# K of a cached attention block loaded by transposing DMAs instead of transposed on TensorE

## The chip, the cores and the metric

One core of one Trainium2 chip runs the whole program. The metric is the device time of one execution in microseconds (us), here the median of the runs shown. A profile of one execution shows what each engine did: TensorE (PE; its weight loads are listed apart as PEld), VectorE (DVE), ScalarE (ACT), GpSimd (POOL), SyncE (SP, which only issues loads), and the 16 DMA engines that move data between HBM and the on-chip memory (SBUF).

## The reference

Two independent blocks A and B of the same shape, whose outputs are laid side by side. In each, 16 batches of 64 queries attend to a cache of 512 keys in 32 heads of 128 dimensions; all data is bf16:

```python
q = (x @ wq).reshape(B, Sq, H, Dh).transpose(0, 2, 1, 3)     # x: 16 x 64 x 640
scores = einsum("bhqd,bhkd->bhqk", q, k_cache) * Dh ** -0.5   # k_cache: 16 x 32 x 512 x 128
p = softmax(scores, axis=-1)
o = einsum("bhqk,bhkd->bhqd", p, v_cache)                     # v_cache: 16 x 32 x 512 x 128
y = o.transpose(0, 2, 1, 3).reshape(B, Sq, H * Dh) @ wo       # wo: 4096 x 640
```

The two caches of the two blocks are the bulk of the traffic: K is 2 x 16 x 32 x 512 x 128 x 2 bytes = 134.2 MB, V as much. The scores need K with the head dimension on the partitions, while the cache holds one key after another.

## The kernel before

A pass is one block and one half of its heads (16 of 32); there are four passes. In a pass the kernel goes over the eight pairs of batches, and within a pair over the 16 heads, two heads at a time. Such a step of two heads (index `m`; the code calls the single head `g`) is the unit of all work: 4 passes x 8 pairs x 8 steps = 256 steps. The two batches of a pair share the 128 rows of a tile, 64 queries each.

One step does, in this order of dependence:

- KX on TensorE (line 433): two groups, one for each batch, of eight transposes of 128x128, from the loaded K tile `kn_ring` into PSUM; KE on VectorE (line 442) copies each group into `ktp_ring`.
- QP2 (line 451): ten matmuls project the two heads' queries from the transposed input; QE2 on ScalarE scales and copies them to `qT_ring`.
- SM2 (line 467): four matmuls, for two heads and two batches, make the scores; their moving operand is 512 columns of `ktp_ring`.
- MX on VectorE (line 476) takes the negated row maximum, EX on ScalarE (line 482) the exponential with its row sum, RC2 on VectorE (line 488) the reciprocal.
- NM on GpSimd (line 496) multiplies by the reciprocal and writes `pn_ring`, permuting the keys on the way: K is loaded with key 8p + t in partition p, V with key 4p + t, so the scores' columns stand in another order than V's rows.
- TR2 (line 505): eight transposes of the probabilities; TE2 on VectorE (line 512) copies them out.
- PV2 (line 524): sixteen matmuls with V; OE2 on ScalarE (line 532) copies out.
- OP2 (lines 540 and 545): the output projection, summed in PSUM over the heads of a pass; its end is added up in line 560 and stored by a DMA on ScalarE's queue (line 566).

The order on each engine is a fixed template that is repeated with the steps: `PE_T`, `ACT_T`, `DVE_T`, `POOL_T`. Each entry has an offset, which says how many steps ahead of the present one it works: TensorE does KX for step k + 4, SM2 for k + 3, TR2 and PV2 for k + 1 and OP2 for k. An engine takes its instructions strictly in that order.

All loads go through one queue, SP's. `build_plan` orders them by when they are needed (its durations `DMA_NS` serve that order alone), and each waits for its buffer to come free. K and V come in chunks of four heads and one batch, 512 KB each (lines 626 and 622), two DMAs for each of them per chunk; a chunk serves two steps. Both have rings of five chunks (`NKB`, `NVB`). A K buffer comes free when the last reader of its chunk, KX before, has passed. K's source is read in runs of eight keys (2 KB), V's in runs of four (1 KB):

```python
# K, lines 624 to 626
src = blocks[blk][1][2 * bp + j, h0 + hlo:h0 + hhi].rearrange("(hp hs) (p t) d -> (hs p) hp t d", hs=2, t=8)
ins = e.dma_start(kn_ring[:, c % NKB, j, hlo // 2:hhi // 2], src)
# V, lines 621 and 622
src = blocks[blk][2][2 * bp + j, h0 + hlo:h0 + hhi].rearrange("g (p t) d -> p g t d", p=128)
ins = e.dma_start(v_ring[:, c % NVB, j, hlo:hhi], src)
```

Of the kernel before, what the change touches and what calls it, by code (L numbers as in the profile page):

```python
# [5 lines left out]
BF16 = mybir.dt.bfloat16  # L6
F32 = mybir.dt.float32
ACTF = mybir.ActivationFunctionType
ALU = mybir.AluOpType
# [5 lines left out]
class Cfg:  # L15
    G = 4
    HH = 16
    NKB = 5
    NVB = 5
    NX = 2  # L20
    NXN = 1
    XLEAD = 10
    NQ = 2
    NKT = 2
    NP = 4
    NPN = 3
    NT = 2
    NO = 2
    NR = 8
    PE_T = (("TR2", 1), ("QP2", 4), ("KX", 4, 0), ("SM2", 3), ("PV2", 1), ("XT", 0), ("OP2", 0), ("KX", 4, 1))  # L30
    ACT_T = (("QE2", 4), ("OE2", 1), ("XE", 0), ("EX", 3, 0), ("EX", 3, 1), ("OV", 0), ("ST", -1))
    DVE_T = (("TE2", 1), ("RC2", 2), ("KE", 4, 0), ("MX", 3, 0), ("MX", 3, 1), ("KE", 4, 1), ("OVF", 0))
    POOL_T = (("NM", 0, 0), ("NM", 0, 1))
    TAIL_SPLIT = 2
    SLOT_NS = 3600.0
# [3 lines left out]
class Op:  # L39
# [3 lines left out]
    def __init__(self, eng, kind, idx, reads=(), writes=(), dur=0.0, ts=None, aux=None):  # L43
# [12 lines left out]
        self.dma = kind in ("LDK", "LDV", "LDX", "LDWQ", "LDWO", "ST")  # L56


STAGES = ("LDW", "LDX", "LDK", "LDV", "KX0", "KE0", "KX1", "KE1", "QP2", "QE2", "SM2", "MX0", "MX1", "EX0", "EX1",
          "RC2", "NM0", "NM1", "TR2", "TE2", "XT", "XE", "PV2", "OE2", "OP2", "OV", "ST")  # L60
STAGE_IDX = {s: i for i, s in enumerate(STAGES)}
SUB_KINDS = ("KX", "KE", "EX", "NM", "MX")


def build_plan(dims, cfg):
    NBLK, B, H = dims["NBLK"], dims["B"], dims["H"]
    G = cfg.G
# [23 lines left out]
    def mk(eng, kind, idx, reads, writes, stage, m_ts, sub=0, aux=None, dur=0.0):  # L91
        return Op(eng, kind, idx, reads, writes, dur=dur, aux=aux, ts=(m_ts, STAGE_IDX[stage], sub))

    OFF = {}
    for t in cfg.PE_T:
        OFF.setdefault(t[0], t[1])

    def make_op(kind, m, sub):
        g0, g1 = 2 * m, 2 * m + 1
        ps_, bp, grp, h0 = step_info(g0)  # L100
        c = g0 // G
        if kind == "KX":
            return mk("pe", "KX", (m, sub), [("kn", c % cfg.NKB, g0 % G), ("kn", c % cfg.NKB, g1 % G), ("ident",)],
                      [("KTB",)], "KX%d" % sub, m, sub)
        if kind == "KE":
            return mk("dve", "KE", (m, sub), [], [("KTB",), ("ktp", m % cfg.NKT, sub)], "KE%d" % sub, m, sub)
        if kind in ("MX", "EX", "NM"):
            g = 2 * m + sub
            r = g % cfg.NR
# [18 lines left out]
        if kind == "QE2":  # L128
            return mk("act", "QE2", m, [], [("QB",), ("qT", m % cfg.NQ)], "QE2", m)
        if kind == "SM2":  # L130
            return mk("pe", "SM2", m, [("qT", m % cfg.NQ), ("ktp", m % cfg.NKT, 0), ("ktp", m % cfg.NKT, 1)],
                      [("SB", 0), ("SB", 1)], "SM2", m)
        if kind == "RC2":
            return mk("dve", "RC2", m, [("rowsum", r0), ("rowsum", r1)], [("recip", r0), ("recip", r1)], "RC2", m)
# [29 lines left out]

    templates = {"pe": cfg.PE_T, "dve": cfg.DVE_T, "pool": cfg.POOL_T, "act": cfg.ACT_T}
    for eng, tmpl in templates.items():
        offs = [t[1] for t in tmpl] + [cfg.XLEAD]
        for k in range(-max(offs), NMAC - min(offs)):
            for t in tmpl:
                kind, off = t[0], t[1]  # L170
                sub = t[2] if len(t) > 2 else 0
                if kind in ("XT", "XE"):
                    op = make_op(kind, k, 0)
# [3 lines left out]
                m = k + off  # L177
                if 0 <= m < NMAC:
                    op = make_op(kind, m, sub)
# [167 lines left out]
def mha_kernel(nc, blocks, out, cfg=None):  # L347
    cfg = cfg or Cfg()
# [14 lines left out]
    prune_waits(progs)  # L363
    NBP, SPB, NHALF = info["NBP"], info["SPB"], info["NHALF"]
    HH = SPB
    NKB, NVB, NX, NXN, NQ, NKT, NP, NPN, NT, NO, NR = (cfg.NKB, cfg.NVB, cfg.NX, cfg.NXN, cfg.NQ, cfg.NKT, cfg.NP,
                                                       cfg.NPN, cfg.NT, cfg.NO, cfg.NR)

    def step_info(g):
        grp = g // SPB  # L370
# [7 lines left out]
    with contextlib.ExitStack() as es:  # L378
        block = es.enter_context(nc.Block())

        def sb(name, shape, dt):
            return es.enter_context(nc.sbuf_tensor(name, shape, dt))
# [15 lines left out]
        negmax = sb("negmax", [128, NR], F32)  # L398
        rowsum = sb("rowsum", [128, NR], F32)
        recip = sb("recip", [128, NR], F32)  # L400
        ones_sb = sb("ones_sb", [128, 128], BF16)
        ident = sb("ident", [128, 128], BF16)
        ps = es.enter_context(nc.psum_tensor("ps", [128, 8, 512], F32))
# [9 lines left out]
        else:  # L413
            out_ps_all = ps[:, 0, 0:DN]
        S_BANK0 = 2
        PT_BANK, O_BANK, Q_BANK, KT_BANK = 4, 5, 6, 7
# [4 lines left out]
        kt_ps_flat = ps[:, KT_BANK, :].bitcast(BF16)  # L421
        kt_ps = kt_ps_flat.rearrange("p (t s) -> p t s", t=8)

        def s_bank(sub):
            return ps[:, S_BANK0 + sub, :]

        def em_KX(e, op):
            m, j = op.idx
            g0 = 2 * m
            c, hp = g0 // G, (g0 % G) // 2  # L430
            first = last = None
            for t8 in range(8):
                ins = e.transpose(kt_ps[:, t8, :], kn_ring[:, c % NKB, j, hp, t8, :], ident[:, :])  # L433
                first = first or ins
                last = ins
            return first, last

        def em_KE(e, op):
            m, j = op.idx
            src = kt_ps_flat.rearrange("p (t hs pp) -> p t hs pp", t=8, hs=2)  # L440
            dst = ktp_ring[:, m % NKT, :, j, :].rearrange("p hs (t pp) -> p t hs pp", t=8)
            ins = e.tensor_copy(dst, src)  # L442
            return ins, ins

        def em_QP2(e, op):
            m = op.idx
# [15 lines left out]
        def em_SM2(e, op):  # L462
            m = op.idx
            first = last = None
            for sub in range(2):
                for j in range(2):
                    ins = e.matmul(s_bank(sub)[64 * j:64 * j + 64, :], qT_ring[:, m % NQ, sub, 64 * j:64 * j + 64],  # L467
                                   ktp_ring[:, m % NKT, sub, j, :], start=True, stop=True, tile_position=(0, 64 * j))
                    first = first or ins
                    last = ins  # L470
            return first, last
# [19 lines left out]
        def em_NM(e, op):  # L491
            g = op.idx
            r = g % NR
            src = p_ring[:, g % NP, :].rearrange("q (th tl pp) -> q th tl pp", th=2, tl=4)
            dst = pn_ring[:, g % NPN, :].rearrange("q (tl pp th) -> q th tl pp", tl=4, th=2)
            ins = e.tensor_scalar(dst, src, recip[:, r:r + 1], 1.0, ALU.mult, ALU.mult)  # L496
            return ins, ins

        def em_TR2(e, op):
# [116 lines left out]
        def em_LDKV(e, op):  # L616
            c, j, hlo, hhi, _piece = op.aux
            blk, bp, grp, ps_, hh0 = step_info(c * G)
            h0 = (ps_ % NHALF) * HH + hh0
            if op.kind == "LDV":  # L620
                src = blocks[blk][2][2 * bp + j, h0 + hlo:h0 + hhi].rearrange("g (p t) d -> p g t d", p=128)
                ins = e.dma_start(v_ring[:, c % NVB, j, hlo:hhi], src)
            else:
                src = blocks[blk][1][2 * bp + j, h0 + hlo:h0 + hhi].rearrange("(hp hs) (p t) d -> (hs p) hp t d",
                                                                              hs=2, t=8)
                ins = e.dma_start(kn_ring[:, c % NKB, j, hlo // 2:hhi // 2], src)  # L626
            return ins, ins

        emitters = dict(KX=em_KX, KE=em_KE, QP2=em_QP2, QE2=em_QE2, SM2=em_SM2, MX=em_MX, EX=em_EX, RC2=em_RC2,
                        NM=em_NM, TR2=em_TR2, TE2=em_TE2, PV2=em_PV2, OE2=em_OE2, OP2=em_OP2, OV=em_OV,  # L630
                        OVP=em_OVP, OVF=em_OVF, ST=em_ST, XT=em_XT, XE=em_XE, INIT1=em_INIT1, INIT2=em_INIT2,
                        LDWQ=em_LDWQ, LDWO=em_LDWO, LDX=em_LDX, LDK=em_LDKV, LDV=em_LDKV)
# [87 lines left out]
```

## Time and profile before

| | |
|---|---|
| median of two runs | 958.89 us (958.25 and 959.54) |
| span of the profiled execution | 956.8 us, so 1.4 to 2.7 us of a run's time lie outside it |
| TensorE busy | 919.4 us |
| VectorE busy | 841.9 us |
| ScalarE busy | 567.1 us |
| GpSimd busy | 416.9 us |
| moved on SP's queue | 294.69 MB, 91.0% of the 16 DMA engines' span |
| K loads | 256 of 512 KB (the last chunk's four halves are 256 KB each), median 7.0 us to landing in block A and 4.8 in B |
| V loads | the same number and sizes, 7.2 and 5.7 us |

Busy times are sums over instructions; TensorE's matmuls are pipelined, so that the sum of their durations is larger than the time in which they follow each other: a group of eight K transposes is busy 0.61 us from its first start to its last end, and starts 0.45 us ahead of whatever follows it. In the groups of instructions the columns are the line, engine and operation, the output and the inputs, the count, the busy time, the mean in ns, and the idle time before them with what ended it. The chain of waits is followed back from the last instruction of the program; its shares tell where the time of the path that ended last went.

### The profile page before, as it was taken

To read this page: it belongs to the slowest core of one execution; us is meant where nothing else is said; L and a number is where in the kernel's file an instruction comes from. 1 tells how busy PE (TensorE), PEld (TensorE's weight loads), DVE (VectorE), ACT (ScalarE), POOL (GpSimd) and SP (SyncE) were. 2 spreads that over 40 slices of the span, in tenths; PEclk is the share of its full clock that TensorE was granted. 3 is DMA by queue.
4 is the path that set the end of the run, shared out by engine and by line. 5 is a ranking of instruction groups with operands and counts; after the bars stand their busy time and mean duration, and the time that the engine had idled before them with its cause. 6 is when DMAs were issued, how large, how long until landed. Compare 5 with 4: busy or idle time off the path is not lost.

```text
span 956.8 us, 34351 instructions
## 1 busy us (share of the span) xinstructions
PE 919.4 (96%) x14755; PEld 733.5 (77%) x15008; DVE 841.9 (88%) x1552; ACT 567.1 (59%) x1585; POOL 416.9 (44%) x518
## 2 busy tenths in 40 slices
PE   4999999999999999999999999999999999999997
PEld 3877777778777777877777787777877778777775
DVE  2898899898899999899999899889899998999996
ACT  1666656666665565656566666666666656565654
POOL 0444444444444444444444444444444444444443
PEclk9999999999999999999999999999999999999999
DMA  9999999999999999888999999988888988899830
GB/s 315 364 365 364 351 365 367 365 368 351 338 337 337 343 330 315 299 292 305 322 332 352 326 353 327 306 294 296 302 305 288 308 301 297 295 297 314 295 124 15
DMA packets 230871, 299.51 MB, mean 313 GB/s; under 512 B 9536, under 2 KB 165184, under 8 KB 230720
## 3 DMA queue, kind: packets, MB, share of 16 engines
q1 hardware_dynamic: 228416, 294.69, 91.0%
q8 instruction: 118, 1.93, 0.8%
q10 hardware_dynamic: 2304, 2.62, 0.8%
q14 instruction: 33, 0.27, 0.1%
HBM read 294.65 MB, written 2.62 MB: 311 GB/s over the span
## 4 chain that ended last, share of the span: by engine, by line
PE 89%; DVE 4%; POOL 3%; issue 2%; SPq 1%; DMA 1%; POOLq 0%; DVEq 0%
PE ps L433 22%; PE ps L524 14%; PE ps L451 14%; PE ps L467 14%; PE ps L505 12%; PE ps L545 7%; PE ps L540 5%; POOL pn_ring L496 3%; DVE out_sb L560 1%; DVE ktp_ring L442 1%; DVE pT_ring L512 1%; PE ps L604 1%; DMA xn_ring<-in_A_x_dram 1%; SPq L626 1%; SPq L583 1%
## 5 line engine op out<-in xcount | busy, mean ns | idle before, releaser
L496 POOL TENSOR_SCALAR pn_ring<-p_ring,recip 128x512 bf16<-128x512 bf16 x512 | 416.3, 843 | 532.7 <-DVE recip L488 532.7
L442 DVE COPY ktp_ring<-ps 128x1024 bf16<-128x1024 bf16 x512 | 353.7, 691 | 105.3 <-PE ps L433 85.1
L482 ACT ACTIVATE p_ring<-ps,negmax 128x512 bf16<-128x512 f32 x512 | 345.6, 684 | 4.8 <-DVE negmax L476 4.8
L476 DVE TENSOR_REDUCE negmax<-ps 128x1 f32<-128x512 f32 x512 | 327.3, 681 | 0.4 <-PE ps L467 0.3
L433 PE MATMUL ps<-ident,kn_ring 128*128 128x128 bf16 x4096 | 314.6, 220 | 2.8 <-DMA kn_ring<-in_A_k_cache_dram 1.6
L532 ACT ACTIVATE oT_ring<-ps 128x256 bf16<-128x256 f32 x256 | 98.0, 383 | 306.0 <-PE ps L524 306.0
L433 PEld LDWEIGHTS ps<-ident,kn_ring 128*128 128x128 bf16 x4096 | 251.9, 98 | 34.2 <-DVE ktp_ring L442 2.6
L524 PEld LDWEIGHTS ps<-pT_ring,v_ring 128*128 128x128 bf16 x4096 | 133.5, 98 | 109.2 <-issue 100.0
L451 PE MATMUL ps<-xT_ring,wq_sb 128*128 128x128 bf16 x2560 | 186.4, 220 | 3.2 <-DMA wq_sb<-in_A_wq_dram 3.2
L512 DVE COPY pT_ring<-ps 128x1024 bf16<-128x1024 bf16 x256 | 174.5, 682 | 4.6 <-PE ps L505 3.8
L524 PE MATMUL ps<-pT_ring,v_ring 128*128 128x64 bf16 x4096 | 163.8, 194 | 3.3 <-issue 1.7
L467 PE MATMUL ps<-ktp_ring,qT_ring 128*64 128x512 bf16 x1024 | 159.8, 392 | 0.4 <-ACT p_ring L482 0.4
L505 PE MATMUL ps<-ident,pn_ring 128*128 128x128 bf16 x2048 | 156.7, 219 | 3.5 <-POOL pn_ring L496 3.5
L451 PEld LDWEIGHTS ps<-xT_ring,wq_sb 128*128 128x128 bf16 x2560 | 155.2, 98 | 3.5 <-DMA wq_sb<-in_A_wq_dram 3.5
L459 ACT ACTIVATE qT_ring<-ps 128x256 bf16<-128x256 f32 x256 | 98.4, 384 | 66.8 <-PE ps L451 66.8
L505 PEld LDWEIGHTS ps<-ident,pn_ring 128*128 128x128 bf16 x2048 | 124.1, 98 | 7.0 <-POOL pn_ring L496 6.7
L545 PE MATMUL ps<-wo_sb,oT_ring 128*128 128x128 bf16 x512 | 112.1, 219 | 13.4
L482 ACT ACTIVATION_READ_ACCUMULATOR p_ring<-ps,negmax 128x1 f32 x512 | 105.0, 205 | 0.0
L540 PE MATMUL ps<-wo_sb,oT_ring 128*128 128x512 bf16 x259 | 97.8, 379 | 0.0
L540 PEld LDWEIGHTS ps<-wo_sb,oT_ring 128*128 128x128 bf16 x512 | 50.1, 98 | 30.6 <-ACT oT_ring L532 0.3
L467 PEld LDWEIGHTS ps<-ktp_ring,qT_ring 128*64 128x64 bf16 x1024 | 36.1, 108 | 27.1 <-ACT p_ring L482 0.6
L545 PEld LDWEIGHTS ps<-wo_sb,oT_ring 128*128 128x128 bf16 x512 | 50.1, 98 | 0.0
(13 smaller groups left out, 112.7 us busy)
## 6 DMA issues: line engine op xcount, KB each, us to landing
kn_ring<-in_A_k_cache_dram SPq DMA_DIRECT2D x128, 512.0 KB, 7.0
v_ring<-in_A_v_cache_dram SPq DMA_DIRECT2D x128, 512.0 KB, 7.2
kn_ring<-in_B_k_cache_dram SPq DMA_DIRECT2D x126, 512.0 KB, 4.8
v_ring<-in_B_v_cache_dram SPq DMA_DIRECT2D x126, 512.0 KB, 5.7
wq_sb<-in_A_wq_dram SPq DMA_DIRECT2D x8, 640.0 KB, 10.4
wo_sb<-in_A_wo_dram SPq DMA_DIRECT2D x8, 640.0 KB, 10.2
wq_sb<-in_B_wq_dram SPq DMA_DIRECT2D x8, 640.0 KB, 8.4
wo_sb<-in_B_wo_dram SPq DMA_DIRECT2D x8, 640.0 KB, 7.5
```

Of the source, the lines that this page charges most:

```text
L433: ins = e.transpose(kt_ps[:, t8, :], kn_ring[:, c % NKB, j, hp, t8, :], ident[:, :])
L442: ins = e.tensor_copy(dst, src)
L451: ins = e.matmul(q_ps[:, sub * 128:(sub + 1) * 128], wq_sb[:, ps_ % 2, kt, hh * DH:(hh + 1) * DH], xT_ring[:, grp % NX, kt, :], start=(kt ...
L467: ins = e.matmul(s_bank(sub)[64 * j:64 * j + 64, :], qT_ring[:, m % NQ, sub, 64 * j:64 * j + 64], ktp_ring[:, m % NKT, sub, j, :], start=T ...
L476: ins = e.reduce_max(negmax[:, r:r + 1], s_bank(g % 2), axis=AX.X, negate=True)
L482: ins = e.activation(p_ring[:, g % NP, :], s_bank(g % 2), ACTF.Exp, bias=negmax[:, r:r + 1], scale=1.0, accum_out=rowsum[:, r:r + 1])
L496: ins = e.tensor_scalar(dst, src, recip[:, r:r + 1], 1.0, ALU.mult, ALU.mult)
L505: ins = e.transpose(pt_ps[:, sub, t, :], pn_ring[:, g % NPN, t * 128:(t + 1) * 128], ident[:, :])
L512: ins = e.tensor_copy(pT_ring[:, m % NT].rearrange("p s t q -> p (s t q)"), pt_ps_flat)
L524: ins = e.matmul(o_ps[:, col:col + 64], v_ring[:, c % NVB, j, gi, t, :], pT_ring[:, m % NT, sub, t, 64 * j:64 * j + 64], start=(t == 0), s ...
L540: ins = e.matmul(out_ps0, oT_ring[:, m % NO, sub, :], wo_sb[:, ps_ % 2, hh, 0:N0], start=(hh == 0), stop=(hh == SPB - 1))
L545: last = e.matmul(out_ps1, oT_ring[:, m % NO, sub, :], wo_sb[:, ps_ % 2, hh, N0:DN], start=(hh == 0), stop=(hh == SPB - 1))
```

## The change

K is loaded by a transposing DMA straight into the layout that the scores need. The source of one DMA is viewed as 512 rows (four heads x 128) of 1 KB, each row four consecutive keys; the destination `kt_ring` has the head dimension on the partitions, and for each of the four positions in a row the 512 rows. So head `gi`'s columns run over (position t, row r) for key 4r + t, which is V's order.

With that, the K transposes (KX) and their copies (KE) go, with the PSUM bank and the ring `ktp_ring` that they used; SM2 reads `kt_ring` directly, as four runs of 128 columns, and waits for the DMA itself; NM writes its result in the order in which it reads it. A K buffer comes free after SM2 (offset 3) instead of KX (offset 4), and the loads are ordered by that. Nothing else in the templates changes.

```diff
-    NKT = 2
+    KR = 128
-    PE_T = (("TR2", 1), ("QP2", 4), ("KX", 4, 0), ("SM2", 3), ("PV2", 1), ("XT", 0), ("OP2", 0), ("KX", 4, 1))
+    PE_T = (("TR2", 1), ("QP2", 4), ("SM2", 3), ("PV2", 1), ("XT", 0), ("OP2", 0))
-    DVE_T = (("TE2", 1), ("RC2", 2), ("KE", 4, 0), ("MX", 3, 0), ("MX", 3, 1), ("KE", 4, 1), ("OVF", 0))
+    DVE_T = (("TE2", 1), ("RC2", 2), ("MX", 3, 0), ("MX", 3, 1), ("OVF", 0))
...
-            return mk("pe", "SM2", m, [("qT", m % cfg.NQ), ("ktp", m % cfg.NKT, 0), ("ktp", m % cfg.NKT, 1)],
+            return mk("pe", "SM2", m, [("qT", m % cfg.NQ), ("kn", c % cfg.NKB, g0 % G), ("kn", c % cfg.NKB, g1 % G)],
...
-        for kind, ring, n_ring, cons, tb in (("LDK", "kn", cfg.NKB, "KX", 2), ("LDV", "v", cfg.NVB, "PV2", 2.5)):
+        for kind, ring, n_ring, cons, tb in (("LDK", "kn", cfg.NKB, "SM2", 2), ("LDV", "v", cfg.NVB, "PV2", 2.5)):
...
+    KR, KJ = cfg.KR, SK // cfg.KR
...
-        kn_ring = sb("kn_ring", [128, NKB, 2, G // 2, 8, DH], BF16)
+        kt_ring = sb("kt_ring", [128, NKB, 2, KJ, G * KR], BF16)
-        ktp_ring = sb("ktp_ring", [128, NKT, 2, 2, SK], BF16)
...
-                ins = e.transpose(kt_ps[:, t8, :], kn_ring[:, c % NKB, j, hp, t8, :], ident[:, :])
...
-            ins = e.tensor_copy(dst, src)
...
+                g = 2 * m + sub
+                c, gi = g // G, g % G
                 for j in range(2):
                     ins = e.matmul(s_bank(sub)[64 * j:64 * j + 64, :], qT_ring[:, m % NQ, sub, 64 * j:64 * j + 64],
-                                   ktp_ring[:, m % NKT, sub, j, :], start=True, stop=True, tile_position=(0, 64 * j))
+                                   kt_ring[:, c % NKB, j, :, gi * KR:(gi + 1) * KR], start=True, stop=True, tile_position=(0, 64 * j))
...
-            src = p_ring[:, g % NP, :].rearrange("q (th tl pp) -> q th tl pp", th=2, tl=4)
-            dst = pn_ring[:, g % NPN, :].rearrange("q (tl pp th) -> q th tl pp", tl=4, th=2)
-            ins = e.tensor_scalar(dst, src, recip[:, r:r + 1], 1.0, ALU.mult, ALU.mult)
+            ins = e.tensor_scalar(pn_ring[:, g % NPN, :], p_ring[:, g % NP, :], recip[:, r:r + 1], 1.0, ALU.mult, ALU.mult)
...
-                src = blocks[blk][1][2 * bp + j, h0 + hlo:h0 + hhi].rearrange("(hp hs) (p t) d -> (hs p) hp t d",
-                                                                              hs=2, t=8)
-                ins = e.dma_start(kn_ring[:, c % NKB, j, hlo // 2:hhi // 2], src)
+                src = blocks[blk][1][2 * bp + j, h0 + hlo:h0 + hhi].rearrange("g (r t) d -> (g r) (t d)", t=KJ)
+                ins = e.dma_start_transpose(kt_ring[:, c % NKB, j, :, hlo * KR:hhi * KR], src)
```

More of the change, by code (lines that the diff above doesn't have):

```diff
@@ L56, in __init__ @@
         self.dma = kind in ("LDK", "LDV", "LDX", "LDWQ", "LDWO", "ST")
-STAGES = ("LDW", "LDX", "LDK", "LDV", "KX0", "KE0", "KX1", "KE1", "QP2", "QE2", "SM2", "MX0", "MX1", "EX0", "EX1",
+STAGES = ("LDW", "LDX", "LDK", "LDV", "QP2", "QE2", "SM2", "MX0", "MX1", "EX0", "EX1",
           "RC2", "NM0", "NM1", "TR2", "TE2", "XT", "XE", "PV2", "OE2", "OP2", "OV", "ST")
 STAGE_IDX = {s: i for i, s in enumerate(STAGES)}
-SUB_KINDS = ("KX", "KE", "EX", "NM", "MX")
+SUB_KINDS = ("EX", "NM", "MX")
 def build_plan(dims, cfg):
@@ L101, in make_op @@
         c = g0 // G
[L102 to L106, printed above, removed]
         if kind in ("MX", "EX", "NM"):
@@ L365, in mha_kernel @@
     HH = SPB
-    NKB, NVB, NX, NXN, NQ, NKT, NP, NPN, NT, NO, NR = (cfg.NKB, cfg.NVB, cfg.NX, cfg.NXN, cfg.NQ, cfg.NKT, cfg.NP,
-                                                       cfg.NPN, cfg.NT, cfg.NO, cfg.NR)
+    NKB, NVB, NX, NXN, NQ, NP, NPN, NT, NO, NR = (cfg.NKB, cfg.NVB, cfg.NX, cfg.NXN, cfg.NQ, cfg.NP,
+                                                  cfg.NPN, cfg.NT, cfg.NO, cfg.NR)
     def step_info(g):
@@ L415, in mha_kernel @@
         S_BANK0 = 2
-        PT_BANK, O_BANK, Q_BANK, KT_BANK = 4, 5, 6, 7
+        PT_BANK, O_BANK, Q_BANK = 4, 5, 6
         pt_ps_flat = ps[:, PT_BANK, :].bitcast(BF16)
@@ L420, in mha_kernel @@
         q_ps = ps[:, Q_BANK, 0:256]
-        kt_ps_flat = ps[:, KT_BANK, :].bitcast(BF16)
-        kt_ps = kt_ps_flat.rearrange("p (t s) -> p t s", t=8)
         def s_bank(sub):
             return ps[:, S_BANK0 + sub, :]
[L427 to L443, printed above, removed]
         def em_QP2(e, op):
@@ L623, in em_LDKV @@
             else:
-                src = blocks[blk][1][2 * bp + j, h0 + hlo:h0 + hhi].rearrange("(hp hs) (p t) d -> (hs p) hp t d",
-                                                                              hs=2, t=8)
-                ins = e.dma_start(kn_ring[:, c % NKB, j, hlo // 2:hhi // 2], src)
+                src = blocks[blk][1][2 * bp + j, h0 + hlo:h0 + hhi].rearrange("g (r t) d -> (g r) (t d)", t=KJ)
+                ins = e.dma_start_transpose(kt_ring[:, c % NKB, j, :, hlo * KR:hhi * KR], src)
             return ins, ins
-        emitters = dict(KX=em_KX, KE=em_KE, QP2=em_QP2, QE2=em_QE2, SM2=em_SM2, MX=em_MX, EX=em_EX, RC2=em_RC2,
+        emitters = dict(QP2=em_QP2, QE2=em_QE2, SM2=em_SM2, MX=em_MX, EX=em_EX, RC2=em_RC2,
                         NM=em_NM, TR2=em_TR2, TE2=em_TE2, PV2=em_PV2, OE2=em_OE2, OP2=em_OP2, OV=em_OV,
```

## The prediction

> **What bounds the kernel now.** I read the page first: busy shares, slices, chain, groups.
>
> ```profile
> span 956.8 us, 34351 instructions
> ...
> PE 919.4 (96%) x14755; PEld 733.5 (77%) x15008; DVE 841.9 (88%) x1552; ACT 567.1 (59%) x1585; POOL 416.9 (44%) x518
> ...
> GB/s 315 364 365 364 351 365 367 365 368 351 338 337 337 343 330 315 299 292 305 322 332 352 326 353 327 306 294 296 302 305 288 308 301 297 295 297 314 295 124 15
> DMA packets 230871, 299.51 MB, mean 313 GB/s; under 512 B 9536, under 2 KB 165184, under 8 KB 230720
> ...
> q1 hardware_dynamic: 228416, 294.69, 91.0%
> ...
> PE 89%; DVE 4%; POOL 3%; issue 2%; SPq 1%; DMA 1%; POOLq 0%; DVEq 0%
> PE ps L433 22%; PE ps L524 14%; PE ps L451 14%; PE ps L467 14%; PE ps L505 12%; PE ps L545 7%; PE ps L540 5%; POOL pn_ring L496 3%; DVE out_sb L560 1%; DVE ktp_ring L442 1%; DVE pT_ring L512 1%; PE ps L604 1%; DMA xn_ring<-in_A_x_dram 1%; SPq L626 1%; SPq L583 1%
> ...
> L442 DVE COPY ktp_ring<-ps 128x1024 bf16<-128x1024 bf16 x512 | 353.7, 691 | 105.3 <-PE ps L433 85.1
> ...
> L433 PE MATMUL ps<-ident,kn_ring 128*128 128x128 bf16 x4096 | 314.6, 220 | 2.8 <-DMA kn_ring<-in_A_k_cache_dram 1.6
> ```
>
> TensorE sets the end: 89% of the chain, its largest line the K transposes, L433. But the loads stand close behind. The slices show some 365 GB/s in the first third and about 300 later, so I next took two stretches as windows (the columns after the busy times are granted clock, DMA share and GB/s):
>
> ```profile
> 100.00:200.00 100.00, 98.53 (x1599) 79.35 (x1626) 89.95 (x168) 62.57 (x175) 44.54 (x56) 1.00 1.07 365
> 700.00:800.00 100.00, 98.03 (x1589) 78.16 (x1614) 90.66 (x169) 59.79 (x169) 44.78 (x56) 1.00 0.89 297
> ```
>
> Early the rings are being filled and the DMA engines give all they have, 365 GB/s at a share above 1. Late they deliver only what TensorE uses. Last, the chain of waits over one steady step, a pair of heads:
>
> ```profile
> 412.93 0.45 PE ps L433 x8
> 413.38 0.45 PE ps L505 x8
> 413.82 0.56 PE ps L451 x10
> 414.38 0.45 PE ps L433 x8
> 414.83 0.55 PE ps L467 x4
> 415.38 0.57 PE ps L524 x16
> 415.95 0.05 issue
> 416.01 0.22 PE ps L545
> 416.23 0.21 PE ps L540
> 416.44 0.06 PE ps L545
> 416.50 0.45 PE ps L433 x8
> ```
>
> One step is 416.50 - 412.93 = 3.57 us, and 256 x 3.57 = 914 us of the 956.8.
>
> **What is removed.** Two groups of eight K transposes, 2 x 0.45 = 0.90 us a step. TensorE alone would need 2.67 us a step, 256 x 2.67 = 684 us, 230 less. VectorE loses L442: 841.9 - 353.7 = 488 us, 1.9 a step; ScalarE needs 567 / 256 = 2.2, GpSimd 417 / 256 = 1.6. All lie below 2.67, so no engine takes TensorE's place. L496 becomes a contiguous normalization; it is the same 512 elements at 843 ns or less or somewhat more, and would have to grow from 1.6 to over 2.67 us a step to matter: nothing. The four score matmuls of L467 read their 512 columns as four runs of 128 instead of one: nothing if the 0.55 us holds, and at worst the pace of L433 (0.45 us for 8 x 128 columns against 0.55 for 4 x 512) says that short runs are not dearer. They now wait for the K landing itself. Queued behind that wait on TensorE are PV, the output projection and the next step, and behind them all evictions; what a late K costs is thus whole, and belongs to the loads below. K buffers come free one step later (scores at offset 3, not transposes at 4), one of the ring's ten steps; with the loads behind, that is not what holds them.
>
> **What takes its place: the loads.** The bytes stay, 294.7 MB on q1. Even at 365 GB/s they need 807 us, more than TensorE's 684. So gain or loss is the price of a transposed byte, which no row of before shows. The trace's DMA packet records give sizes and durations. Medians: 4 B 9 ns (9537 of them), 1024 B 46 ns (V and Wq, 141312), 1280 B 55 ns (x, Wo and stores, 14336), 2048 B 84 ns (K, 65536). They lie on a line: (84 - 46) / 1024 = 0.037 ns per byte, plus 8 ns per packet. Over 16 engines:
> - all but K: (141312 x 46 + 14336 x 55) / 16 = 406 + 49 = 455 us
> - K now: 65536 x 84 / 16 = 344 us.
> Together 799 us, against 807 from the saturated rate: the medians price the load within 1%, and I multiply sums by 1.01.
>
> K's 134.2 MB, transposed, has these prices:
> - **as whole 1 KB source rows** at V's price: 131072 x 46 / 16 = 377 us.
> - **as 256 B pieces.** A head dimension is 128 x 2 B = 256 B. In a 1 KB row four keys stand side by side, and the destination puts them in four different groups, so a row must be cut in four for the transposition. By the line, 8 + 0.037 x 256 = 17.5 ns each, 524288 x 17.5 / 16 = 573 us.
> - **as small writes.** If the destination were served in 32 B pieces at the 9 ns of the smallest packets: 4194304 x 9 / 16 = 2359 us.
>
> The lower end is 344 (nothing lost against now), the upper 2359. I take 573: it is next to the 1 KB and 2 KB rows on the same line, while the upper end has only the 4 B row behind it.
>
> Sum: (455 + 573) x 1.01 = 1038 us of loading. Ends: 1 us before the first issue, 2 for the last landing (the shortest K landing, 3.6 us, less 512 KB at 365 GB/s, 1.4), and the last chunk's work: two steps of about 3.2 at the end of the trace and 5.0 from the last PV (951.8) to 956.8, so 11. That is 1052 of span. Outside the span lie 958.9 - 956.8 = 2.1, so **1054 us**. TensorE then idles 1052 / 256 - 2.67 = 1.4 us a step.
>
> The Trainium skill, "Advanced Engine Details and Errata", section "X-Bar Transpose (TRN2)", states the contrary: transposing DMAs as fast as plain ones, 350 to 400 GB/s; with it K would take 336 to 383 us and the kernel 815 to 862. "DMA: Bandwidth & Descriptors", section "Latency and other measured facts", gives 261 GB/s where a middle dimension is not contiguous, as in these rows; that estimate is 514 us for K and 995 in all. Neither is shown by the trace.
>
> SP issues each transfer. The issues of K (256 packets) and V (512 packets) both take 0.37 us when nothing holds them, so packet count does not show in it. Were the issue to grow as pieces do (2048 against 512), it would be 1.5 us; per chunk 2 x 1.5 + 2 x 0.37 = 3.7 us, hidden under the 8.1 us that a chunk's loads then take. Before,
>
> ```profile
> SPq L626 <- PE ps L433: 353.5, 119, 4.0
> ```
>
> SP waited 353.5 us for TensorE to free K buffers; that wait goes, and SP is held by the DMA engines instead, as in 100 to 200 us. V, Wo and x stand behind K in the same queue, and are late with it.
>
> **Rivals.**
> *Rows move whole* (faster): K at 377. (455 + 377) x 1.01 + 16 = 856 us. For it: 1 KB runs already move at 46 ns for V. Against: the four keys of a row part on the way. It wins under the point where K takes 460 us, 14.0 ns per 256 B piece or 292 GB/s: that gives 940, 2% below 958.9.
> *Something between* (890 to 985): part of the piece's 8 ns is overlapped. The band within 2%, about what a measurement of this kernel can tell from no change, is K between 460 and 498 us.
> *Each transposing DMA drains the engines* before the next transfer starts. 3.6 - 1.4 = 2.2 us of latency exposed, x 256 = 563: 856 + 563 = 1419 or 1054 + 563 = 1617. For it: nothing shown; against it: plain transfers overlap freely (share 1.07).
> *Small writes*: (455 + 2359) x 1.01 + 16 = 2858.
> *A slow TensorE*: after the 4.2 us for which the matmuls stood still before 23.3 us a group of eight transposes took 1.03 us instead of 0.61, until 27 us. At that ratio a step is 2.67 x 1.69 = 4.5 us, 1153 in all. But it cannot stay: at 4.5 against the loads' 4.05 us a step TensorE would never idle, and the pace returned after some 4 us of work. It adds at most at stalls, inside the range.
> *No effect of the removal*: excluded, L433 and L442 are gone by the diff and nothing replaces them on an engine.
>
> The skill's "VectorE: DVE Perf Modes", section "Rules for kernel authors", speaks against the change: for 128 x 128 use TensorE where PSUM will do, the crossbar otherwise; its table has 1309 ns for one by DMA. The 4096 blocks one after another would make 5362 us as an estimate; the trace, with 0.45 us per eight on TensorE, can't say how far DMAs overlap them.
>
> **How the numbers follow.** 256 B pieces, 985 to 1110: 0.33, the likeliest. Whole rows, 835 to 890: 0.26. Between, 890 to 985: 0.12, of it 0.05 faster than 940, 0.06 within 2% and 0.01 slower. Drained, 1110 to 1620: 0.19. Small writes and other steep prices above that: 0.10. Faster is 0.26 + 0.05 = 0.31, same 0.06, slower 0.33 + 0.01 + 0.19 + 0.10 = 0.63. The range goes from 840 to 1560 and leaves out the steep prices, the upper edge of the drained case (0.05) and a little below (0.02). The forecast's own range is 985 to 1110.
>
> **What would show it.** Right: no L433 and L442; packets of 256 B on q1 near 17.5 ns; DMA share 0.9 or more in all slices at 270 to 300 GB/s; the chain mostly DMA into kt_ring and TensorE's busy time near 919 - 315 x 0.73 = 690 (0.73 is the chain's 0.90 us a step over the 1.23 that 314.6 / 256 gives). Wrong: K packets of 1 KB at 46 ns (whole rows); a DMA share far below 0.9 while TensorE waits for K (drained, or SP as the limit, which its issue durations would show); hundreds of thousands of packets under 64 B (small writes).

## The result, and the profile after

The changed kernel takes **1224.94 us** (1223.66 to 1226.22, two runs) against 958.89: ratio 1.278, interval 1.274 to 1.282. It is slower, as forecast, but by 266 us where 95 were forecast. Where the executions of a kernel fall into a faster and a slower state, the times and ratios below are of the faster ones.

From the page of the changed kernel: span, busy times, granted clock, DMA share and GB/s in 40 slices, DMA packets, two DMA queues, and the chain of waits.

```profile
span 1221.9 us, 25784 instructions
...
PE 847.0 (69%) x10784; PEld 586.6 (48%) x10912; DVE 551.0 (45%) x1040; ACT 553.7 (45%) x1585; POOL 350.1 (29%) x518
...
PEclk9878888888888878888988887988888888888888
DMA  9999999999999999999999999999999999999997
GB/s 229 260 244 236 266 251 239 248 247 245 246 259 263 246 253 243 264 238 255 249 240 254 245 244 244 262 240 228 254 237 243 236 237 264 235 253 236 238 248 168
DMA packets 693715, 298.97 MB, mean 245 GB/s; under 512 B 537952, under 2 KB 693600, under 8 KB 693600
...
q1 hardware_dynamic: 691296, 294.70, 107.8%
...
q8 instruction: 86, 1.41, 0.5%
...
SPq 40%; DMA 28%; PE 19%; ACT 9%; issue 2%; POOL 1%; DVE 0%; POOLq 0%; ACTq 0%; DVEq 0%
SPq L600 34%; DMA v_ring<-in_B_v_cache_dram 12%; DMA v_ring<-in_A_v_cache_dram 10%; ACT p_ring L459 7%; PE ps L444 6%; PE ps L499 6%; SPq L597 4%; DMA kt_ring<-in_B_k_cache_dram 3%; DMA kt_ring<-in_A_k_cache_dram 3%; PE ps L426 2%; PE ps L480 2%; PE ps L515 2%; ACT oT_ring L507 2%; SPq L572 1%; ACT xT_ring L587 1%
```

The chain has passed from TensorE to the loads: 40% SP's queue (L600 issues K), 28% DMA. The packets under 512 B are the 256 B pieces. The DMA engines are never without work (share 1.08) and yet carry 245 GB/s. The share adds up the durations of packets, which overlap, and does not say that the engines move all they can: before, a share of 1.07 went with 365 GB/s. SP's issues in order of time (start, duration, operation, destination and source, count):

```profile
304.97 7.88 SPq L600 DMA_TRANSPOSE kt_ring<-in_A_k_cache_dram  x2
312.89 1.13 SPq L597 DMA_DIRECT2D v_ring<-in_A_v_cache_dram  x2
314.06 7.74 SPq L600 DMA_TRANSPOSE kt_ring<-in_A_k_cache_dram  x2
```

SP issues almost without a pause, a transposing DMA holding it some 4 us, and a chunk takes 9 us. The waits of SP's queue name TensorE as what it waits for, 249 us in 92 waits:

```profile
SPq L600 <- PE ps L444: 249.1, 92, 5.4
```

That is an inferred releaser, and wrong here. Set against the end of the last scores that read the buffer, SP's issue of a K load comes 27 to 36 us later (10th to 90th percentile; 24 at the least), of a V load 33 to 39 us later. The buffers are free long before. TensorE in turn uses V 6.2 us (median) after the issue of a chunk's first V load starts, and a V load takes 5.2 us to land. So the stream of loads sets the time, and its sum is what went wrong.

### The profile page after: what moved, and what is told of

Read it like the earlier page. It is cut to its first block, busy times and chain, and to the rows that moved or that the text cites. A ratio compares the mean times of both kernels' runs of the same rounds, so it can differ in the third digit from the quotient of the medians.

```text
span 1221.9 us, 25784 instructions
## 1 busy us (share of the span) xinstructions
PE 847.0 (69%) x10784; PEld 586.6 (48%) x10912; DVE 551.0 (45%) x1040; ACT 553.7 (45%) x1585; POOL 350.1 (29%) x518
## 4 chain that ended last, share of the span: by engine, by line
SPq 40%; DMA 28%; PE 19%; ACT 9%; issue 2%; POOL 1%; DVE 0%; POOLq 0%; ACTq 0%; DVEq 0%
SPq L600 34%; DMA v_ring<-in_B_v_cache_dram 12%; DMA v_ring<-in_A_v_cache_dram 10%; ACT p_ring L459 7%; PE ps L444 6%; PE ps L499 6%; SPq L597 4%; DMA kt_ring<-in_B_k_cache_dram 3%; DMA kt_ring<-in_A_k_cache_dram 3%; PE ps L426 2%; PE ps L480 2%; PE ps L515 2%; ACT oT_ring L507 2%; SPq L572 1%; ACT xT_ring L587 1%
## 5 line engine op out<-in xcount | busy, mean ns | idle before, releaser
L471 POOL TENSOR_SCALAR pn_ring<-p_ring,recip 128x512 bf16<-128x512 bf16 x512 | 349.4, 695 | 864.6 <-DVE recip L465 864.6
L499 PE MATMUL ps<-pT_ring,v_ring 128*128 128x64 bf16 x4096 | 188.9, 205 | 263.0 <-DMA v_ring<-in_A_v_cache_dram 131.1
L444 PE MATMUL ps<-kt_ring,qT_ring 128*64 128x512 bf16 x1024 | 174.8, 424 | 70.1 <-ACT p_ring L459 34.6
L426 PE MATMUL ps<-xT_ring,wq_sb 128*128 128x128 bf16 x2560 | 214.5, 239 | 5.3 <-DMA wq_sb<-in_A_wq_dram 4.9
L480 PE MATMUL ps<-ident,pn_ring 128*128 128x128 bf16 x2048 | 186.4, 243 | 9.9 <-ACT xT_ring L587 8.4
L426 PEld LDWEIGHTS ps<-xT_ring,wq_sb 128*128 128x128 bf16 x2560 | 182.4, 109 | 6.7 <-issue 3.3
L480 PEld LDWEIGHTS ps<-ident,pn_ring 128*128 128x128 bf16 x2048 | 147.6, 111 | 66.5 <-POOL pn_ring L471 20.2
L515 PE MATMUL ps<-wo_sb,oT_ring 128*128 128x512 bf16 x384 | 160.4, 452 | 0.0
L444 PEld LDWEIGHTS ps<-kt_ring,qT_ring 128*64 128x64 bf16 x1024 | 38.7, 113 | 113.1 <-ACT p_ring L459 72.3
L465 DVE RECIPROCAL recip<-rowsum 128x2 f32<-128x2 f32 x256 | 41.6, 162 | 7.4 <-ACT p_ring L459 1.4
```

The source lines that it names most:

```text
L426: ins = e.matmul(q_ps[:, sub * 128:(sub + 1) * 128], wq_sb[:, ps_ % 2, kt, hh * DH:(hh + 1) * DH], xT_ring[:, grp % NX, kt, :], start=(kt ...
L471: ins = e.tensor_scalar(pn_ring[:, g % NPN, :], p_ring[:, g % NP, :], recip[:, r:r + 1], 1.0, ALU.mult, ALU.mult)
L480: ins = e.transpose(pt_ps[:, sub, t, :], pn_ring[:, g % NPN, t * 128:(t + 1) * 128], ident[:, :])
L499: ins = e.matmul(o_ps[:, col:col + 64], v_ring[:, c % NVB, j, gi, t, :], pT_ring[:, m % NT, sub, t, 64 * j:64 * j + 64], start=(t == 0), s ...
L515: ins = e.matmul(out_ps0, oT_ring[:, m % NO, sub, :], wo_sb[:, ps_ % 2, hh, 0:N0], start=(hh == 0), stop=(hh == SPB - 1))
```

## The experiments

Before the runs the theories were: **boundaries**, time lost where the DMA engines pass between transposing and plain transfers; **each transposing DMA**, a price for every one; **strided pieces**, 256 B reads at steps of 1 KB being slow; **coupling**, engines and queue holding each other up. Later came **instruction fetch** and **SBUF traffic**.

### The loads alone

All computing is left out and zeros are stored; SP issues the same loads in the same order, each waiting only for the landing of the load that filled its buffer before. Each time in this part and the next is of one execution.

```diff
-            run_program(sync, progs["sp"])
+            for op in loads:                      # the same list, op.waits: the buffer's earlier load
+                for s, v in op.waits:
+                    e.wait_ge(sems[s], v * 16)
+                _, ins = emitters[op.kind](e, op)
+                ins.then_inc(sems[op.sem], 16)
```

**Plain K**, the list of the kernel before:

> The loads of the kernel before alone, in its order on SP's queue: all computing is left out, each load waits only for the landing of the load that filled its buffer before, and zeros are stored at the end. A gauge for the other three. Every theory: 294.7 MB at the 365 GB/s of the filled stretch, 807 us and about 15 at the ends, 820 us.

Measured 823.7 us. The price list of the prediction, 455 + 344 at the medians, multiplied by 1.01 and with the ends, holds for plain loads.

**Alternating**, the list of the changed kernel:

> The loads of the changed kernel alone, K by transposing DMAs, K and V alternating as there; all computing left out, zeros stored. At the medians of the packet records (18 ns for 256 B, 46 for 1 KB, 56 for 1280 B) the engines need 590 + 406 + 50 = 1046 us; the changed kernel's span is 1222, so 176 us are to be placed. Theory 'boundaries' (time is lost where the DMA engines pass between transposing and plain transfers): about 1210 us. Theory 'each transposing DMA' (something at the start or end of every one): about 1210. Theory 'strided pieces' (256 B read at steps of 1 KB stall in HBM): about 1210. Theory 'coupling' (TensorE's waits for V and SP's waits for K buffers hold each other up, and a slower granted clock): about 1060.

Measured 1168.4 us. Coupling falls: without any computing most of the excess is there.

**Separated**, `loads = [all but LDK] + [all LDK]`:

> The same loads alone with K by transposing DMAs, but all plain loads first and then all K loads: one passage between the kinds instead of some 256. Boundaries: 1050 to 1070 us. Each transposing DMA: about 1210, and K's part about 590 + 176 = 770 us for 256 DMAs, 3.0 us each. Strided pieces: about 1210 too. Coupling: the same as the alternating loads.

Measured 1072.5 us, 96 less. The GB/s in 40 slices, of the separated run:

```profile
GB/s 310 350 351 350 349 349 351 351 349 349 350 352 349 349 349 349 348 236 214 217 216 213 215 213 210 219 224 213 216 236 235 242 232 234 236 242 240 236 231 237
```

and of the alternating one:

```profile
GB/s 228 278 251 261 241 256 262 257 242 249 254 240 255 254 259 250 238 246 255 238 266 270 254 264 257 256 269 246 247 253 252 259 249 275 259 260 269 259 256 264
```

The first 17 slices are plain loads at 350; after the break K comes alone at 210 to 242. By the packet records K takes 599 us (from 461 to 1060), 2.34 us for each 512 KB. In a quarter of a microsecond up to some 285 of its packets start, 14.0 ns per packet and engine, which would be 1.80 us a DMA. So 0.54 us of each is lost inside the K stream, and 96 us more by alternating.

The packet records also show where. K's packets were counted in order of their start, 2048 to a DMA, and the time of each 64 compared with the peak pace, 56.5 ns. In the alternating run a transposing DMA behind V loses 0.94 us, all of it in its first 640 packets; the second of the two, behind another K, loses 0.61 us, of which 0.51 there. In the separated run it is 0.50 us a DMA. So the loss stands at the start of each transposing DMA, and the start is dearer behind V: 256 x (0.77 - 0.50) = 69 of the 96 us.

**Rows of 256 B** (`KR = 512`, so keys in another order than V's; alternating):

> The loads alone, alternating, K by transposing DMAs whose source rows are 256 B (2048 rows a DMA, one key each) instead of 1 KB: the same bytes and pieces, read in order of address. Strided pieces: the loss goes, 1050 to 1070 us or less. Boundaries, and each transposing DMA: unchanged against the 1 KB rows, within 2%. If SP's issue grows with the rows (2048 instead of 512), it is slower than with 1 KB rows.

Measured 1161.7 us, 0.6% below the 1 KB rows. Strided pieces fall, and SP's issue does not grow with the rows (medians 3.51 and 2.88 us in the two blocks, against 3.57 and 2.72).

**One K, one V** (`K0 V0 K1 V1` instead of `K0 K1 V0 V1`):

> The loads alone (computing left out), as in the alternating run of 1168 us, but passing between K and V after every DMA instead of every two: 512 passages between the kinds in the order of issue instead of 260. With all plain loads first it was 1072, so 96 us for 260 passages, 0.37 us each. Boundaries: 512 x 0.37 = 190, about 1262 us. If the 96 us come from something else than the number of passages (the length of what is queued, or the loads of x and the weights between them): 1168 within 2%.

Measured 1137.0 us: no sign of the 94 us more that a fixed price per passage asks for. That it is 31 us less is not shown to come from the order (see the copies below).

**Four K, four V** (the loads of two chunks together):

> The loads alone, with the loads of two chunks together: four of K, then four of V, 128 passages between the kinds instead of 260. If a passage has its price (96 us for 260): 1072 + 47 = 1120 us. If the engines run further apart in a longer run of V and that is what costs (512 passages took 1137): 1168 or more.

Measured 1123.4 us: as a price per passage has it. Against the separated order this is 51 us at 128 passages, 96 at 260 and 65 at 512; the last, with only one V load between two K loads, does not lie on their line.

**Chunks of eight heads**, DMAs of 1 MB:

```diff
-    G = 4
+    G = 8
-    NKB = 5
-    NVB = 5
+    NKB = 2
+    NVB = 2
```

> The loads alone in chunks of eight heads: DMAs of 1 MB, half as many, and two buffers for each of K and V; the order is two K, two V, so passages and bytes between them are as in the order of four and four with 512 KB. Within the K stream of the separated run a DMA took 2.34 us, of which 1.80 at its peak rate. Theory 'each transposing DMA' (0.54 us lost at every one): 128 fewer, 69 us less than the run with four and four. Theory 'along the stream' (the loss goes with bytes): the same time as that one, within 2%.

Measured 1040.0 us, 83 less than four and four, for the same bytes between passages: 83 / 128 = 0.65 us for each transposing DMA saved. This is the clearest of the experiments on the stream. The V loads are half as many too, but the packet records put the loss with K: a 1 MB DMA loses 0.71 us against the peak pace, 0.64 of it in the first 640 of its 4096 packets, where the 512 KB DMAs of four and four lose 0.65. The price is one of the start, and not of the bytes.

**V from ScalarE's queue**:

> The loads alone, with V issued from ScalarE's queue and all others, K's transposing DMAs among them, from SP's, so that both kinds are in flight on every DMA engine at once. If a passage costs because one ring must run empty: 1072 us or less, down to 875, which is the sum of both kinds at their peak rates (285 packets of 256 B in 0.25 us and 94 of 1 KB). If transposing DMAs need all 16 engines in step and every plain packet between them holds all up: 1168 us or more.

Measured 1020.3 us. Between 20 and 520 us V and K packets start one for one (132,000 of each), at 350 GB/s in all; which engine carried which the records don't say. But nothing held V back, so that it ran ahead and the rest was K alone: nearly the separated order. I read it as support for "one ring in order", which the whole kernel then refuted (below).

### What computing adds: 1168 to 1225

**11000 small matmuls beside the alternating loads**:

```diff
+        def _(t):
+            for i in range(11000):
+                t.matmul(ps[0:128, 0, 0:128], ident[:, :], ident[:, :], start=True, stop=True)
```

> The alternating loads alone, with 11000 small matmuls beside them on TensorE whose operands are one constant tile that no load touches: some 22000 instructions to be fetched, as in the changed kernel, and no other work. In the changed kernel's packet records the 256 B packets fall from 0.87 to 0.13 of their full rate for some 1.2 us when an instruction fetch of 16 KB (86 on queue 8) begins. Theory 'instruction fetch' (a fetch holds one DMA engine and a transposing DMA waits for all 16): 1168 + 86 x 0.6 to 0.9 = 1220 to 1245 us. Theory 'coupling' (the 57 us between 1168 and 1225 come from SP and TensorE waiting for each other): 1168 within 1%. Theory 'SBUF traffic': 1168 within 1%.

Measured 1213.1 us, with 86 fetches on queue 8. The matmuls end at 619 us, so the run is its own control. Windows (TensorE, its weight loads and GpSimd with counts, granted clock, DMA share, GB/s):

```profile
40.00:240.00 200.00, 200.00 (x3586) 200.00 (x3584) 0.00 (x0) 1.00 1.13 244
240.00:440.00 200.00, 200.00 (x3586) 200.00 (x3584) 0.00 (x0) 1.00 1.14 235
...
660.00:860.00 200.00, 0.00 (x0) 0.00 (x0) 0.00 (x0) 0.50 1.07 257
860.00:1060.00 200.00, 0.00 (x0) 0.00 (x0) 0.00 (x0) 0.50 1.08 254
```

The rate is 235 to 244 GB/s with the matmuls and 254 to 257 without; the alternating loads alone had 256 and 250 in the first two of these windows, 255 and 259 in the last two. Against its own second part the run so loses some 35 us (6% of 620), though the alternating loads too are 2% slower in the first windows; against the total of the alternating run it is 45.

**22000 waits on a raised semaphore instead of the matmuls** (fetches, no access to SBUF):

> The alternating loads alone, with 22000 waits on a semaphore that has long been raised as the only instructions on TensorE: instructions are fetched as in the run with 11000 matmuls (1213 us), and no engine touches SBUF. Instruction fetch: 1168 + 45 = 1213 us again, with about 86 packets of 16 KB on queue 8. If the 45 us came from TensorE's reads of SBUF: 1168 within 1%.

Measured 1201.0 us, with only 43 fetches (the trace has some 11,000 of the waits). The total alone decides nothing, but the packet records do: averaged over the fetches, q1 falls from 265 GB/s in the microsecond before a fetch to 136 between 0.5 and 1.75 us after its start. Beside the matmuls it falls from 277 to 97. As no engine touches SBUF here, TensorE's reads of SBUF are not what stops the loads.

**Large copies by VectorE, ScalarE and GpSimd**:

> The alternating loads alone, with VectorE, ScalarE and GpSimd copying large tiles inside SBUF that no load touches, 1680 instructions of 1 to 2 us in all, so few fetches. SBUF traffic (the compute engines' accesses slow the transposed writes): 1200 us or more. Instruction fetch and coupling: 1168 within 1.5%.

Measured 1514.5 us, but that is VectorE's copies, which go on long after the loads: the last V packet starts at 1128 us of the span, where it was 1156 in the alternating run. SBUF traffic of these three engines doesn't slow the loads. The 29 us by which they came in *below* are also a warning: single runs of the alternating loads differ by some 2 to 3%, so that the 31 us of one K, one V and the 33 of the waits are not shown by their totals alone. One K, one V ran on the same chip as these copies, the run of 1168 us on another. Its last V packet starts at 1125 us against their 1128, so that on one chip the two orders come out alike.

The changed kernel's own trace shows the same. One of the fetches begins at 305.1 us; the DMA view of 305 to 308 us, in 40 slices of 75 ns:

```profile
GB/s 492 280 273 266 273 257 185 27 31 34 41 41 27 27 14 0 3 7 10 20 24 10 10 7 10 10 24 273 355 437 341 205 0 314 314 369 355 341 369 314
...
q1 hardware_dynamic: 874, 0.46, 103.3%
q8 instruction: 1, 0.02, 2.5%
```

One 16 KB packet, on one of 16 engines, and the end of a transposing DMA with the V load behind it falls from 270 to between 0 and 41 GB/s for 1.5 us. Averaged over all 86 fetches, q1 falls from 259 to 92 GB/s between 0.5 and 1.75 us after the start. Over the run, with each packet counted at its kind's peak rate, the engines do 0.49 of their peak work from 0.25 us before to 2.5 us after the start of a fetch and 0.78 elsewhere: 85 us at 85 fetches. In the kernel before, between 20 and 300 us, where the DMA engines are full too, it is 0.87 and 0.89: 2 us at 34 fetches. The net effect on the total is smaller than those 85, some 35 to 45 us at 86 fetches in the run with matmuls.

### The whole kernel

**One K, one V:**

> The whole changed kernel, with the loads of a chunk issued K, V, K, V instead of K, K, V, V. In the landing records the 16 engines end a V load some 0.6 to 0.8 us apart and a transposed K load 0.2 apart; a transposing DMA behind plain ones would have to wait until the last engine is through. Theory 'in step' (the loss at a passage grows with how far the engines have run apart, so half as much V between two K loads costs less in all): as in the loads alone (1168 to 1137), 31 us less than 1225, 1194. Theory 'boundaries' (a price for each passage): 1225 + 96 = 1320. If the two runs of loads alone differed by chance: 1225 within 1%.

Measured 1263.5 us, ratio to the kernel before 1.317 (1.312 to 1.321): slower by 39 us where the loads alone had been no slower. All three expectations miss it, and it stays open.

**V from ScalarE's queue** (`op.eng = "act"`, issued after OE2 of the buffer's last step):

> The whole changed kernel with V issued from ScalarE's queue (after the eviction of the last PV step that read the buffer) instead of SP's. In the loads alone V's 1 KB and K's 256 B packets then alternated one to one on each engine at 355 GB/s in all, with no gaps, and the loads took 1020 us instead of 1168. Theory 'one ring in order' (the passages lose time only where both kinds stand in the same ring): 1020 and 45 for the instruction fetches, 1065 to 1080 us. Theory 'in step however issued': 1225 or more. If ScalarE, held in the issue of V, becomes late for its evictions: above 1100.

Measured 1228.3 us (1224.1 and 1232.4), ratio 1.281 (1.276 to 1.287): no different from the changed kernel's 1225. A second queue does not help when V is held to the pace of K; "one ring in order" falls. ScalarE late for its evictions would fit the time too, but in the chain of this kernel's profile ScalarE has 8%, DMA 36% and SP's queue 32%.

**Four K, four V:**

> The whole changed kernel in that order, four K and then four V. SP's issues come 25 us and more after their buffers are free, so the order makes no engine wait for a buffer. Price of a passage: 1225 - 49 = 1176 us. Engines apart: 1225 or more. If what is lost is tied to single transposing DMAs, whose number stays: 1225 within 1.5%.

Measured 1197.3 us, ratio 1.250 (1.248 to 1.252): 28 less, where 49 were expected of a price per passage.

**DMAs of 1 MB** (`G = 8`, `NKB = 3`, `NVB = 2`):

> The whole changed kernel in chunks of eight heads, so with 128 transposing DMAs of 1 MB instead of 256 of 512 KB, with three buffers for K and two for V (five of half the size before). Alone, these loads took 1040 us against 1123 for the same order of bytes with 512 KB. Theory 'each transposing DMA': the whole kernel in groups of four 512 KB loads took 1197, so 1197 - 83 = 1114 us. If in the whole kernel something else bounds the loads (as one K, one V was faster alone and slower in the kernel): 1197 within 2%. If two buffers for V hold SP up: more than that.

Measured 1141.8 us, ratio 1.192 (1.190 to 1.194): 55 less than with 512 KB, so 0.43 us per transposing DMA in the whole kernel against 0.65 alone, and 83 less than the changed kernel. What the two buffers for V cost in it is not separated.

**A share of the chunks transposed by DMA**, the rest on TensorE as before:

```diff
+    def kt(c):
+        return c % cfg.KF == cfg.KF - 1 and c != NCHUNK - 1
...
+        if kind in ("KX", "KE") and kt(c):
+            return None
```

with the matching loads, scores and normalization for each kind. Every fourth chunk:

> The kernel before with every fourth chunk of K (31 of 128) loaded by transposing DMAs as in the change, and the other three transposed on TensorE as before. TensorE: 957 - 31 x 2 x 0.90 = 901 us. Loads: 822 for plain ones and (1168 - 822) / 128 = 2.7 us more for each transposed chunk, 822 + 84 = 906, and up to 20 for fetches. If both bounds hold and the rings smooth them: 905 to 925, 4 to 5% faster than before. If late transposed K stalls TensorE each time: 950 or more.

Measured 976.4 us, ratio 1.019 (1.017 to 1.021): 1.9% slower. Its chain is TensorE to 60%, DMA to 10% and SP's queue to 9%, so late loads already have a part in it. Every sixth:

> The same with every sixth chunk (21 of 128) transposed by DMA. TensorE: 957 - 21 x 2 x 0.90 = 919 us. Loads: 822 + 21 x 2.7 = 879. So TensorE bounds it: 919 to 930 us, a little slower than with every fourth if the loads of that one hold, faster if they do not.

Measured **949.8 us, ratio 0.991 (0.989 to 0.992)**: 0.9% below the kernel before, less than the 2% within which the forecast speaks of no change, and some 20 us above what was expected. Every eighth:

> The kernel before with every eighth chunk of K (15 of 128) loaded by transposing DMAs. TensorE: 957 - 15 x 2 x 0.90 = 930 us of span at the least. Every sixth (21) took 948.5, every fourth (31) 973: where the loads bound it, 2.5 us for each more; carried down to 15 that is 933. So 933 to 942, ratio 0.975 to 0.985, if these are the two bounds. If what is lost per chunk is TensorE waiting for each late K (1.4 us with every sixth): 951, ratio 0.993.

Measured 951.6 us, ratio 0.992 (0.991 to 0.993), as with every sixth. TensorE isn't waiting for K here (under 5 us in all for K's DMAs). The chain of waits at a transposed chunk of this kernel (start, duration):

```profile
414.75 0.63 PE ps L528 x8
415.39 0.02 issue
415.41 0.69 DVE pT_ring L535
416.10 0.08 DVE recip L509
416.18 0.08 issue
416.27 1.64 POOL pn_ring L519 x2
417.90 0.05 issue
417.95 0.62 PE ps L528 x8
```

A step without K transposes is not 2.67 us long but 417.95 - 414.75 = 3.20: the transposes of the probabilities, their eviction, the reciprocal behind it on VectorE, the two normalizations on GpSimd, and the next transposes form a loop. So such a step gains 3.57 - 3.20 = 0.37 us instead of 0.90, 15 x 2 x 0.37 = 11 us with every eighth chunk, which from 956.8 gives 946 against the span of 949.8. To shorten the loop (the reciprocal ahead of the eviction on VectorE) wasn't tried.

## Why the prediction was wrong

**The bound and the direction** were right: TensorE gives way to the loads, L433 and L442 go, and DMA and SP's queue make the chain. Of the signs named, the share of 0.9 or more came, but with 245 GB/s in place of 270 to 300: the share didn't tell that time was lost.

**The piece** was right: K moves in 524288 packets of 256 B with a median of 18 ns, where 17.5 were read off the line through the packets of before. That K alone took 599 us where (573 x 1.01) 579 stood is luck, though. At their peak the packets follow each other every 14.0 ns, which makes 459 us, and the starts, 0.54 us for each of 256 DMAs, add 138. A pace that was 114 us too slow stood in for a price of the start that was missing. 134.2 MB in 599 us is 224 GB/s against 350 for plain loads. The Trainium skill, "Advanced Engine Details and Errata", section "X-Bar Transpose (TRN2)", has transposing DMAs as fast as regular ones; here they are not, and the measurement decides.

**The step that failed** is the sum, "(455 + 573) x 1.01 = 1038 us of loading". It takes the two kinds of loads as adding up without loss between them. The 1.01 was the kernel before's, whose plain transfers run on with no gap from one to the next; it was carried over to transfers that do not. The loads alone took 1072 us separated and 1168 in the order of the kernel. The price of starting a transposing DMA was set at nothing in the forecast and at 2.2 us each in the rival "each transposing DMA drains the engines". By the packet records it is 0.5 to 0.6 us behind another transposing DMA and 0.94 behind V; the DMAs of 1 MB against 512 KB give 0.65 us alone and 0.43 in the whole kernel. So the mechanism stood among the rivals and its size was between: the row that the prediction took for it, the shortest landing less the transfer, measures the full latency of a load, and most of that is overlapped. The time lies in the band of that rival, 1110 to 1620.

**What was left out:** the instruction fetches, a term that the forecast doesn't have, 35 to 45 us by the run with matmuls. Put together: 1072 separated, 96 for alternating, 35 to 45 for fetches make 1204 to 1214 of 1225. Each of these terms is a difference of single runs, and the 2 to 3% by which such runs differ are as large as the last of them. The last V load is followed by 10 us of work, where 11 were forecast.

**A stage with another limit was priced by one engine.** "TensorE alone would need 2.67 us a step" missed the loop of 3.20 us. It was in view: the ends of the forecast use steps "of about 3.2 at the end of the trace", where no K transposes are left. In the changed kernel, whose two normalizations take 1.37 us instead of 1.64, the same loop would be some 2.9 us by these rows, an estimate. With the loads at 4.77 us a step it cost this forecast nothing; for the mixed kernels it was most of the expected gain.

**Smaller points.** The normalization fell from 843 to 695 ns, and the four short runs of the score matmuls cost nothing (0.62 us for the group of four, as before, at the full clock). TensorE's busy time is 847 us instead of about 690, in part since its clock was granted at half in stretches (0.873 in the mean; a transpose of L480 takes 243 ns, of L505 before 219). The rival "a slow TensorE" was right that this doesn't hold the loads up, as the 24 us and more between a buffer's release and its next load show. The prediction has SP's issue of a transposing DMA at 1.5 us at most; it takes 1.6 us at the shortest and 3.9 to 4.0 in the median. Most of that is waiting, since the same issue can be short; whether a start is slow because of the DMA engines or because of the issue is not separated by these runs.

**Open:** what makes the first packets of a transposing DMA slow, and slower behind V; why one K, one V is slower in the whole kernel; the split of the last 11 to 21 us.

## What to carry to other kernels

Price a new kind of transfer not by its packets alone but with a start for each transfer (here 0.4 to 0.9 us for each transposing DMA, so few large ones), and ask what stands ahead of it in the queue. Before counting on the time that a removed step frees, look in the same trace for a stretch where the step is already missing: its pace is the next limit. Where two resources are both near their bound, moving a small share of the work can be all that pays: here a sixth gained 0.9%, where moving all of it lost 28%.

## What the runs showed of the hardware

The 16 parts of a transposing DMA land nearly together. In the landing records the first and last part of one load are 1.40 us apart for K and 1.59 for V (medians) in the kernel before; in the changed one 0.22 us for K and 0.55 for V. With that goes the effect of an instruction fetch: a packet of 16 KB on one engine, about 1.1 us long, takes the traffic of all 16 from 259 to 92 GB/s for 1.25 us, while full plain traffic hardly shows it (357 to 350). That the one follows from the other is argued, not shown.

A transposing DMA of 512 KB or 1 MB is slow above all in its first 640 packets and then runs at 14.0 ns per packet of 256 B and engine, 292 GB/s. With 512 KB the start costs 0.5 to 0.6 us behind another transposing DMA and 0.94 behind plain loads.

Packets of both kinds do start one for one when they come from two queues and nothing holds V back, at 350 GB/s in all.
